# Three score sets of a head pair as two or three stretches of TensorE, and other ranks in the planner

## Chip, cores and metric

One core of one Trainium2 chip runs the whole program in one launch. The metric is the device time of that launch in microseconds (us); below, a lower number is a faster kernel. Engines: PE is TensorE, PEld its weight loads, DVE is VectorE, ACT is ScalarE, POOL is GpSimd, SP is SyncE, which issues the DMAs.

## The reference

Causal attention with a decay, 4 batches x 8 heads, 576 positions, 64 wide, all in float32; then a token mix and a channel mix with residuals; then a gated convolution. Cut to what is computed:

```python
scores = scale * np.matmul(q, k.transpose(0, 1, 3, 2))
cum = np.cumsum(np.log(np.clip(f, 0.0001, 1.0)), axis=-1)
scores = np.where(causal, -1e9, scores + cum[..., :, None] - cum[..., None, :])
attn = softmax(scores)                                   # rows of 576
x = matmul(attn, v)                                      # (4, 576, 512) after joining the heads
u = x + (np.maximum(x.T @ w_tok1, 0.0) @ w_tok2).T       # 256 wide
x2 = u + np.maximum(u @ w_ch1, 0.0) @ w_ch2              # 1536 wide
h = np.maximum(x2 @ w_in, 0.0)                           # 1024 wide
out = (h * sigmoid(conv3(h, conv_w))) @ w_out
```

## The kernel before, in words

**An order made by a planner.** Nearly all work is handed to `Order.add` (called `T`) as tasks: engine, an estimated duration, a rank, the function that emits the instructions, what it reads and writes, and the PSUM banks it holds (`ring`). `Order.run` plays the tasks through with these estimates. Each engine takes, of the tasks that are ready first, the one with the lowest rank; a rank decides only between tasks that are ready at the same moment. The order that comes out is the order of instructions in each engine's queue, and on the chip each engine works through its queue strictly in that order. Two kinds of PSUM bank are planned: `z` (two, each of two banks) and `w` (four).

**Heads and pairs.** 32 heads are taken in 16 pairs (`pair`, L1126). The ranks of head n lie at n x PER; PER is a number of ranks, not a time. For a pair, `score` (L964) makes the scores in five blocks of query rows (0 to 4, with 64 to 576 columns of keys), the two heads on the two halves of TensorE's rows. They come in three sets: block 4 alone (two z banks, one for each head), blocks 0 and 3 (one z bank for both heads), blocks 1 and 2 (one). In each, the products (L987) are followed by the decay (L991). `smax` (L1005, VectorE) adds the mask and takes the maximum out of a z bank, `sexp` (L1011, ScalarE) the exponential. The banks of block 4 come free with the two heads' `smax` of block 4. In the kernel before, the set of blocks 0 and 3 takes two z banks at once, its own and that of blocks 1 and 2, and the latter set has rank -1e6, so that it follows directly.

**After the scores.** Heads 0 to 7 are transposed by TensorE in float32 (L1044) and multiplied with v in float32 (L1076). From head 8 on the probabilities are split into two float16 halves (L1020 on GpSimd, L1026 on VectorE), transposed by DMA, and multiplied with v in three float16 products (L1081 to L1083). Head 31 goes by TensorE again. `norm` and `xout` (L1088 to L1099) divide by the sums; `x_hi`, `x_lo` make float16 halves.

**Groups and batches.** Four heads are a group: the token mix (`t1`, `t2`, three products at L280 to L282, with transposes at L1228), then a copy and the largest value (L266). Two groups are a batch: its scale (L237 on) is found, and u is split in halves (L591, L594). Then `channel_mix` of part 0 (5 of 12 blocks of 128 channels) for the batch's two chunks may run: first product `w<-uh,w`, halves `r` (L643, L647; nine buffers), second product `w<-r,w`. Its TensorE tasks have ranks of 1000 and more, so they fill what attention leaves. The other 7 blocks, and the gated convolution, run after attention.

**Weights.** Each weight block is loaded, joined from two words (L317 on ScalarE, L321 and L322 on VectorE), squared (L517), and when its set's scale is known, split into halves (L551 on ScalarE, L555 on VectorE). Two staging buffers, `wraw`, are used in the order in which the program names the blocks: token weights t1 (3) and t2 (4), then `c10` (5 blocks of w_ch1) and `c20` (5 of w_ch2) of part 0, then the later sets. TOKR, TOKP, VRANK, SETR, LATER and AVAIL are ranks of these: SETR those of c10 and c20, relative to AVAIL[0] - 30.

Of the kernel before, what the change touches and what calls it, by code (L numbers as in the profile page):

```python
# [143 lines left out]
def fox_moe_kernel(  # L144
# [16 lines left out]
    B, S, H, _ = v.shape  # L161
# [44 lines left out]
    LAST = 1  # L206
    BY_PE = [n < TURNED or n >= NH - LAST for n in range(NH)]

    TOKR, TOKP = 4.0, 5.0
    VRANK = 10.0  # L210
    SETR = ((-15.0, 20.0),)
    LATER = (-60.0, 0.0, 20.0)
    PER = 7.0

    const = ctx.enter_context(tc.tile_pool(name="const", bufs=1))
    work = ctx.enter_context(tc.tile_pool(name="work", bufs=1))
# [68 lines left out]
    pools = {}  # L285
# [12 lines left out]
    T = todo.add  # L298
    serial = [0]

    def turn(tag):

        serial[0] += 1
        return (tag, serial[0])
# [443 lines left out]
    with tc.manual_schedule():  # L748
# [153 lines left out]
        def v_scales(g, rank, reads, pools_):  # L902
            kw = turn("w")
            T("ACT", 1.27, rank, v_squares, g, reads=reads, writes=[("junk",), ("vacc", g % 2)], pools=pools_)
            T("PE", 0.25, rank, v_span, g, reads=[("vacc", g % 2)], writes=[kw], pools=["a1"], ring=[kw])
            T("DVE", 0.7, rank, v_pow, g, reads=[kw], writes=[("vsc", g % 3)], pools=["a1"], ring=[kw])

        def v_tasks(g, rank):
# [4 lines left out]
            if HG * g < FULL:  # L913
                if g:
                    T("SP", 2.0, rank - 6, load_v32, g, writes=keys, moved=3.0, pools=["a3"])
                v_scales(g, rank + VRANK, keys, ["a3", "a1"])
                return
# [41 lines left out]

        SETS = {(4,): DEC4, (0, 3): 0, (1, 2): DEC12}  # L960

        JOINED = ((0, 3), (1, 2))

        def score(p, blocks):  # L964
            t = qk_t[p % QKB]
            halves = [slice(64 * x, 64 * x + 64) for x in range(2)]
# [153 lines left out]
        def x_scale(n):  # L1120
            nc.gpsimd.tensor_scalar(x_of(n), x_of(n), tac[:, 0:1], 0.0, ALU.mult, ALU.add)

        PE_S = {(4,): 1.65, (0, 3): 1.25, (1, 2): 1.25}
        DVE_S = {4: 0.81, 3: 0.69, 2: 0.56, 1: 0.42, 0: 0.29}
        ACT_E = {4: 0.78, 3: 0.67, 2: 0.56, 1: 0.46, 0: 0.34}
        SEG = ((4, 3), (2, 1, 0))  # L1126
# [1 line left out]
        def pair(p):  # L1128
            t0 = 2 * p * PER
            kq = ("qk", p % QKB)  # L1130
            A2, A3, A1 = ["a2"], ["a2", "a3"], ["a1"]
            if p:
                T("SP", 0.4, t0 - 9, load_qk, p, writes=[kq], moved=2.6, pools=A2)
            for blocks in SETS:
                second = blocks == JOINED[1]
                kz = [turn("z") for _ in range(2 if blocks == (4,) else 1)] if not second else [kj]
                if blocks == JOINED[0]:
                    kj = turn("z")
                T("PE", PE_S[blocks], -1e6 if second else t0 + 1, score, p, blocks, reads=[kq], writes=[*kz, ("scores",)],
                  pools=A2 + A1, ring=kz + [kj] if blocks == JOINED[0] else kz)  # L1140
                for x, i in ((x, i) for x in range(2) for i in blocks[::-1]):
                    n = 2 * p + x
                    kt = ("t", n % TB)
                    rank = t0 + x * PER
                    T("DVE", DVE_S[i], rank + 2, smax, n, i, reads=[kz[x % len(kz)]], writes=[(*kt, i), ("m", n % 3, i)],
                      pools=A2 + A1, ring=[kz[x % len(kz)]])
                    T("ACT", ACT_E[i], rank + 3, sexp, n, i, reads=[("m", n % 3, i)], writes=[(*kt, i)], pools=A2)
            for n in (2 * p, 2 * p + 1):
                rank = n * PER
                kt = ("t", n % TB)  # L1150
                g = n // HG
                if BY_PE[n]:
                    for a, blks in enumerate(QUADS):
# [3 lines left out]
                          writes=[kw, ("pth", n % 2, a), ("ptl", n % 2, a)], pools=A2 + A1, ring=[kw])  # L1157
                        if n < FULL:
                            T("DVE" if a == 2 else "ACT", 0.14 + 0.115 * len(blks), rank + 4, ptr_copy, n, a, reads=[kw],
                              writes=[("pth", n % 2, a), ("ptl", n % 2, a)], pools=A2 + ["a3"], ring=[kw])  # L1160
                            continue
                        T("ACT", 0.15 + 0.12 * len(blks), rank + 4, ptr_hi, n, a, reads=[kw], writes=[("pth", n % 2, a)],
                          pools=A2 + ["a3"], ring=[kw])
                        T("DVE", 0.12 + 0.17 * len(blks), rank + 4, ptr_lo, n, a, reads=[kw, ("pth", n % 2, a)],
                          writes=[("ptl", n % 2, a)], pools=A2 + ["a3"], ring=[kw])
                else:
                    for q in range(2):
                        T("POOL", (1.22, 1.05)[q], rank + 4, hi_part, n, q, reads=[(*kt, i) for i in SEG[q]],
                          writes=[("ph", n % 2, q)], pools=A2)
                    T("SP", 1.5, rank + 5, transp, n, 0, reads=[("ph", n % 2, 0), ("ph", n % 2, 1)],  # L1170
                      writes=[("pth", n % 2, a) for a in range(len(QUADS))], moved=2.5, pools=A3)
                    for q in range(2):
                        T("DVE", (1.35, 0.9)[q], rank + 4, lo_part, n, q,
                          reads=[(*kt, i) for i in SEG[q]] + [("ph", n % 2, q)], writes=[("pl", n % 2, q)], pools=A2)
                    T("SP", 1.5, rank + 5, transp, n, 1, reads=[("pl", n % 2, 0), ("pl", n % 2, 1)],
                      writes=[("ptl", n % 2, a) for a in range(len(QUADS))], moved=2.5, pools=A3)
# [3 lines left out]
                for i in ORDER:  # L1180
                    T("PE", (0.22 if n < FULL else 0.1) * len(PVB[i]), rank + 6, pv, n, i, reads=[*kp, *vk], writes=[kw, ("xf", g % 2, n % HG)],
                      pools=["a3"], ring=[kw])
# [4 lines left out]
                  writes=[("xl", n % HG)], pools=A1)  # L1187
# [25 lines left out]
        for j in range(NS):  # L1213
            s0, n = (0, 64) if j == 0 else (64 + 128 * (j - 1), 128)
# [60 lines left out]
        def group(g):  # L1275
            t0 = (HG * g + HG - 1) * PER + 6
            A1 = ["a1"]
# [55 lines left out]
        W1K = [("tokw", "t1", k) for k in range(3)]  # L1333
        W2K = [("tokw", "t2", k) for k in range(2 * KT)]
        v_tasks(0, -8)
        AVAIL = [(H * (b + 1) - 1) * PER + 40 for b in range(B)]
        LATE = 1000.0
        tpw = []
        for name, ws, slots, q, factor in (("t1", tok_w[:3], (9, 10, 11), TOKR, 4.0),
                                           ("t2", tok_w[3:], (9, 10, 11, 12), TOKR + 15.0, 2.0 ** 13)):  # L1340
            n = len(ws)
# [8 lines left out]
        T("DVE", 0.2, TOKR + 15.0 + TOKP * 4, tok_scales, reads=[("pw", "t1"), ("pw", "t2")], writes=[("tac",)], pools=["a1"])  # L1350
        t0 = AVAIL[0] - 30
        at = 0
        for x in range(EARLY):
            n = PARTS_M[x]
            for y, (name, w, factor) in enumerate((("ch1", w_ch1, 4.0), ("ch2", w_ch2, 2.0 ** 13))):
                ms = range(M_AT[x], M_AT[x + 1])
                q = t0 + SETR[x][y]
                pw = weight_set(f"c{y + 1}{x}", [(name, m, (col_block if y == 0 else row_block)(w, m)) for m in ms],
                                list(range(at, at + n)), at - 1 if at else 2 * M1,
                                [q + 2.0 * k for k in range(n)], [q + 2.0 * n + 2.0 * k for k in range(n)], factor)  # L1360
                if y == 0:
                    pws.append([pw])
                else:
                    pws[-1].append(pw)
                at += n
        rts1 = ("r1", 9, [0])

        for g in range(NG):
            for p in range(HG * g // 2, HG * (g + 1) // 2):
                pair(p)  # L1370
            if g + 1 < NG:
                v_tasks(g + 1, (HG * g + 2) * PER)
            group(g)
            if g % GB == GB - 1:
                b = g // GB
                for e in range(2):
                    channel_mix(2 * b + e, 0, AVAIL[b] + e * 14, early_u[2 * b + e], None, rts1, "w", "w", LATE, -20.0)

# [36 lines left out]
        for x in range(EARLY, len(PARTS_M)):  # L1415
            n = PARTS_M[x]
            ms = range(M_AT[x], M_AT[x + 1])
            q = T_END + LATER[x - EARLY]
            pws.append([])
# [7 lines left out]
        for b in range(B):  # L1427
            q = T_2 + 2 * P2 * b
# [182 lines left out]
```

## Time and profile before

| | us |
|---|---|
| median of 3 runs | 718.52 (717.6 to 718.86) |
| the profiled execution, device time | 717.27 |
| its span, first to last instruction | 715.5 |
| TensorE busy in the span | 695.6 (97%) |
| VectorE busy | 506.0 (71%) |
| ScalarE busy | 427.8 (60%) |
| GpSimd busy | 242.3 (34%) |

The busy time of an engine is the time in which at least one of its instructions runs. A timeline row gives the start, the duration, the engine, the line and the operation, what it writes and reads, and in square brackets the idle time ahead of it with what ended it. Matmuls overlap in their records, so what one costs is read from start to start. Shares over the whole span mix stages with different limits; the rows below are by stage.

### The profile page before, as it was taken

To read this page: it belongs to the slowest core of one execution; us is meant where nothing else is said; L and a number is where in the kernel's file an instruction comes from. 1 tells how busy PE (TensorE), PEld (TensorE's weight loads), DVE (VectorE), ACT (ScalarE), POOL (GpSimd) and SP (SyncE) were. 2 spreads that over 40 slices of the span, in tenths; PEclk is the share of its full clock that TensorE was granted. 3 is DMA by queue.
4 is the path that set the end of the run, shared out by engine and by line. 5 is a ranking of instruction groups with operands and counts; after the bars stand their busy time and mean duration, and the time that the engine had idled before them with its cause. 6 is when DMAs were issued, how large, how long until landed. Compare 5 with 4: busy or idle time off the path is not lost.

```text
span 715.5 us, 16392 instructions
## 1 busy us (share of the span) xinstructions
PE 695.6 (97%) x6417; PEld 560.0 (78%) x6417; DVE 506.0 (71%) x1264; ACT 427.8 (60%) x939; POOL 242.3 (34%) x321
## 2 busy tenths in 40 slices
PE   6999888999999999999999999999999999999998
PEld 5889665778877787888888778778878778778786
DVE  5787889989987688446566857435778866875570
ACT  5988776685766545545574544112177766676671
POOL 2247563749363657230000212103023222323240
PEclk9999999999999999999999999999999999999999
DMA  8445869799995969784465864345211111100101
GB/s 209 158 128 166 205 196 258 112 256 242 229 233 149 188 137 214 211 267 134 145 197 130 267 217 146 97 134 160 65 42 59 51 59 35 60 18 26 35 17 51
DMA packets 152973, 101.98 MB, mean 143 GB/s; under 512 B 89984, under 2 KB 145024, under 8 KB 152896
## 3 DMA queue, kind: packets, MB, share of 16 engines
q1 hardware_dynamic: 152896, 100.94, 54.0%
q8 instruction: 50, 0.82, 0.5%
q14 instruction: 27, 0.22, 0.1%
HBM read 57.73 MB, written 23.59 MB: 114 GB/s over the span
## 4 chain that ended last, share of the span: by engine, by line
PE 88%; DVE 7%; ACT 2%; issue 1%; SPq 1%; POOL 1%; DMA 0%; ACTq 0%; POOLq 0%; DVEq 0%
PE w L280 15%; PE w L281 15%; PE w L282 15%; PE z L281 8%; PE z L280 8%; PE z L282 8%; PE z L987 6%; PE w L1076 3%; PE w L1228 2%; PE w L1044 2%; DVE pl L1026 2%; PE z L991 1%; PE w L260 1%; DVE ul L594 1%; PE w L1082 1%; PE w L1081 1%
## 5 line engine op out<-in xcount | busy, mean ns | idle before, releaser
L280 PEld LDWEIGHTS <-w 128*128 128x128 f16 x1280 | 125.2, 98 | 34.6 <-issue 2.4
L282 PEld LDWEIGHTS <-w 128*128 128x128 f16 x1280 | 125.5, 98 | 33.8 <-issue 1.9
L281 PEld LDWEIGHTS <-w 128*128 128x128 f16 x1280 | 125.2, 98 | 32.8 <-issue 1.7
L280 PE MATMUL w<-uh,w 128*128 128x288 f16 x416 | 119.6, 288 | 2.0 <-ACT uh L591 1.1
L281 PE MATMUL w<-ul,w 128*128 128x288 f16 x416 | 119.7, 288 | 1.7 <-DVE ul L594 1.7
L282 PE MATMUL w<-uh,w 128*128 128x288 f16 x416 | 119.6, 288 | 0.0
L275 POOL TENSOR_TENSOR g<-sg,g 128x286 f16<-128x286 f32 (+1 forms) x64 | 55.0, 866 | 150.6 <-ACT g L269 149.7
L1511 DVE SCALAR_TENSOR_TENSOR cv<-hp,cw,cv 128x286 f32<-128x286 f32 (+1 forms) x128 | 75.6, 598 | 38.4 <-ACT cv L1505 36.2
L1011 ACT ACTIVATE t<-t,m 128x192 f32<-128x192 f32 (+4 forms) x160 | 82.2, 553 | 15.7 <-DVE m L1005 14.3
L643 ACT ACTIVATE r<-w 128x288 f16<-128x288 f32 x96 | 39.1, 407 | 86.7 <-PE w L282 86.0
L1005 DVE CUSTOM_DVE_ANT_0 t<-z,mask 128x192 f32<-128x192 f32 (+4 forms) x160 | 70.3, 479 | 13.7 <-PE z L991 13.3
L720 POOL TENSOR_TENSOR p<-p,u 128x288 f32<-128x288 f32 x32 | 26.7, 864 | 149.1 <-DMA p<-p_d 89.7
L647 DVE SCALAR_TENSOR_TENSOR r<-w,r 128x288 f16<-128x288 f32 x96 | 43.4, 453 | 45.3 <-ACT r L643 45.0
L281 PE MATMUL z<-g,w 128*128 128x286 f16 (+1 forms) x256 | 73.3, 286 | 0.0
L280 PE MATMUL z<-g,w 128*128 128x286 f16 (+1 forms) x256 | 73.0, 285 | 0.0
L282 PE MATMUL z<-g,w 128*128 128x286 f16 (+1 forms) x256 | 72.9, 285 | 0.0
L280 PE MATMUL w<-vh,w 128*128 128x288 f16 x224 | 64.1, 286 | 0.0
L281 PE MATMUL w<-vl,w 128*128 128x288 f16 x224 | 64.1, 286 | 0.0
L282 PE MATMUL w<-vh,w 128*128 128x288 f16 x224 | 64.1, 286 | 0.0
L280 PE MATMUL z<-r,w 128*128 128x288 f16 x224 | 64.1, 286 | 0.0
L281 PE MATMUL z<-r,w 128*128 128x288 f16 x224 | 64.1, 286 | 0.0
L282 PE MATMUL z<-r,w 128*128 128x288 f16 x224 | 64.1, 286 | 0.0
(200 smaller groups left out, 1678.2 us busy)
## 6 DMA issues: line engine op xcount, KB each, us to landing
wraw<-in_moe_w_ch_dram SPq DMA_DIRECT2D x24, 512.0 KB, 4.5
qk<-in_qk_dram SPq DMA_DIRECT2D x16, 608.0 KB, 5.1
u_d<-us SPq DMA_DIRECT2D x8, 576.0 KB, 3.3
p_d<-res SPq DMA_DIRECT2D x32, 144.0 KB, 3.0
p<-p_d SPq DMA_DIRECT2D x8, 576.0 KB, 5.1
u<-u_d SPq DMA_DIRECT2D x8, 576.0 KB, 4.9
x_d<-p SPq DMA_DIRECT2D x8, 576.0 KB, 3.1
u<-x_d SPq DMA_DIRECT2D x8, 576.0 KB, 3.9
```

The lines of the kernel that those rows point to most:

```text
L275: nc.gpsimd.tensor_tensor(o, a, b, ALU.subtract)
L280: nc.tensor.matmul(ps, wh, xh, start=(first and i == 0), stop=False)
L281: nc.tensor.matmul(ps, wh, xl, start=False, stop=False)
L282: nc.tensor.matmul(ps, wl, xh, start=False, stop=(last and i == n - 1))
L643: nc.scalar.activation(out=t[:, 0, :], in_=box["z", m], func=AF.Relu)
L647: nc.vector.scalar_tensor_tensor(t[:, 1, :], box["z", m], 0.0, f32(t[:, 0, :]), ALU.max, ALU.subtract)
L720: nc.gpsimd.tensor_tensor(box["p"][:, d], box["p"][:, d], box["u"][:, d], ALU.add)
L987: nc.tensor.matmul(out_[x], t[r, Q0[i]:Q0[i] + 128], t[r, k0:k0 + n], start=first, stop=False)
L1005: nc.vector.tensor_tensor_reduce(to, z_t.pop((n, i)), mk, -0.125, 3e38, ALU.add, ALU.min, m_t[n][0:rows, i:i + 1])
L1011: nc.scalar.activation(out=tt[0:rows, o:o + w], in_=tt[0:rows, o:o + w], func=AF.Exp, bias=m_t[n][0:rows, i:i + 1], scale=-1.0)
L1076: nc.tensor.matmul(o[:, 0:65], p32(n)[:, 128 * blk:128 * blk + 128], vp32_t[g % 2][:, slot, hh, :], start=(j == 0), stop=(j == nb - 1))
L1511: nc.vector.scalar_tensor_tensor(cv, hp_t[m][:, s0 + t:s1 + t], cw[:, t, m:m + 1], cv, ALU.mult, ALU.add)
```

## The change

The set of blocks 1 and 2 loses its rank of -1e6 and the set of blocks 0 and 3 its claim on a second bank: each set is a task of the same rank with its own bank or banks. The planner's estimates for the two sets become 1.5 and 1.4 instead of 1.25 and 1.25. The ranks of token weights, v, weight sets, late sets and heads become other numbers. No instruction is added or taken away.

```diff
-    TOKR, TOKP = 4.0, 5.0
-    VRANK = 10.0
-    SETR = ((-15.0, 20.0),)
-    LATER = (-60.0, 0.0, 20.0)
-    PER = 7.0
+    TOKR, TOKP = 10.0, 4.0
+    VRANK = 14.0
+    SETR = ((-25.0, 20.0),)
+    LATER = (-20.0, 0.0, 20.0)
+    PER = 6.0
...
-        JOINED = ((0, 3), (1, 2))
...
-        PE_S = {(4,): 1.65, (0, 3): 1.25, (1, 2): 1.25}
+        PE_S = {(4,): 1.65, (0, 3): 1.5, (1, 2): 1.4}
...
             for blocks in SETS:
-                second = blocks == JOINED[1]
-                kz = [turn("z") for _ in range(2 if blocks == (4,) else 1)] if not second else [kj]
-                if blocks == JOINED[0]:
-                    kj = turn("z")
-                T("PE", PE_S[blocks], -1e6 if second else t0 + 1, score, p, blocks, reads=[kq], writes=[*kz, ("scores",)],
-                  pools=A2 + A1, ring=kz + [kj] if blocks == JOINED[0] else kz)
+                kz = [turn("z") for _ in range(2 if blocks == (4,) else 1)]
+                T("PE", PE_S[blocks], t0 + 1, score, p, blocks, reads=[kq], writes=[*kz, ("scores",)], pools=A2 + A1,
+                  ring=kz)
...
-        AVAIL = [(H * (b + 1) - 1) * PER + 40 for b in range(B)]
+        AVAIL = [(H * (b + 1) - 1) * PER + 35 for b in range(B)]
...
-                                [q + 2.0 * k for k in range(n)], [q + 2.0 * n + 2.0 * k for k in range(n)], factor)
+                                [q + 2.5 * k for k in range(n)], [q + 2.5 * n + 2.5 * k for k in range(n)], factor)
```

## Rows read from the trace of the kernel before

**Rows 1.** The page: its head, and engines' shares of the chain that ended last.

```profile
span 715.5 us, 16392 instructions
...
PE 88%; DVE 7%; ACT 2%; issue 1%; SPq 1%; POOL 1%; DMA 0%; ACTq 0%; POOLq 0%; DVEq 0%
```

**Rows 2.** By stretch: its length, busy us of PE, PEld, DVE, ACT, POOL; clock, DMA.

```profile
16.00:84.00 68.00, 67.22 (x576) 59.02 (x572) 52.32 (x186) 58.67 (x135) 33.22 (x48) 1.00 0.52 160
84.00:120.00 36.00, 27.55 (x256) 19.76 (x252) 32.72 (x81) 24.56 (x49) 17.18 (x21) 0.91 0.88 209
120.00:300.00 180.00, 178.26 (x2180) 143.27 (x2177) 150.71 (x414) 112.53 (x235) 102.09 (x107) 1.00 0.92 197
300.00:712.00 412.00, 412.00 (x3365) 329.25 (x3363) 261.48 (x560) 222.97 (x505) 84.74 (x116) 1.00 0.35 108
```

**Rows 3.** Timeline of TensorE, 84 to 120 us: starts after idle time; last, pair 6.

```profile
87.76 0.37 PE L281 MATMUL w<-xl,w1h 128*128 128x256 f16 x1 [1.27 <-POOL xl L275]
...
106.49 0.28 PE L280 MATMUL w<-uh,w 128*128 128x288 f16 x1 [1.10 <-ACT uh L591]
...
116.88 1.25 PE L987 MATMUL z<-qk 64*128 64x64 f32 x8 [0.93 <-DVE m L1005]
...
118.99 1.13 PE L987 MATMUL z<-qk 64*128 64x192 f32 x8 [0.63 <-DVE m L1005]
```

**Rows 4.** Timeline of TensorE around the joined stretch of pair 9.

```profile
169.00 0.29 PE L281 MATMUL w<-r,w 128*128 128x288 f16 x1
169.13 0.29 PE L282 MATMUL w<-r,w 128*128 128x288 f16 x1
169.34 1.25 PE L987 MATMUL z<-qk 64*128 64x64 f32 x8
...
170.66 1.03 PE L987 MATMUL z<-qk 64*128 64x192 f32 x8
...
171.84 0.28 PE L280 MATMUL w<-xh,w1h 128*128 128x256 f16 x1
```

**Rows 5.** Timeline of TensorE around the stretch of block 4 of pair 9.

```profile
161.86 0.20 PE L1082 MATMUL w<-vp,pt 128*128 128x64 f16 x1
161.89 0.19 PE L1083 MATMUL w<-vp,pt 128*128 128x65 f16 x1
162.02 1.24 PE L987 MATMUL z<-qk 64*128 64x288 f32 x8
...
163.45 0.30 PE L280 MATMUL w<-uh,w 128*128 128x288 f16 x1
```

**Rows 6.** Timeline of VectorE: the two maxima of block 4, pairs 8 and 9.

```profile
154.29 0.75 DVE L1005 CUSTOM_DVE_ANT_0 t<-z,mask 128x576 f32<-128x576 f32 x1
...
154.96 0.75 DVE L1005 CUSTOM_DVE_ANT_0 t<-z,mask 128x576 f32<-128x576 f32 x1
...
164.38 0.74 DVE L1005 CUSTOM_DVE_ANT_0 t<-z,mask 128x576 f32<-128x576 f32 x1
...
168.52 0.74 DVE L1005 CUSTOM_DVE_ANT_0 t<-z,mask 128x576 f32<-128x576 f32 x1
```

**Rows 7.** Timeline of the weight loads around the joined stretch of pair 9.

```profile
169.01 0.10 PEld L282 LDWEIGHTS <-w 128*128 128x128 f16 x1
169.34 0.52 PEld L987 LDWEIGHTS z<-qk 64*128 64x128 f32 x8 [0.24 <-issue]
```

**Rows 8.** Timeline of VectorE: first and last of c10's five low halves.

```profile
81.80 0.74 DVE L555 SCALAR_TENSOR_TENSOR w<-w,pw_c,w 128x512 f16<-128x512 f32 x1
...
94.40 2.27 DVE L555 SCALAR_TENSOR_TENSOR w<-w,pw_c,w 128x512 f16<-128x512 f32 x1
```

**Rows 9.** Timeline of VectorE: the last of c20's five low halves.

```profile
137.62 0.74 DVE L555 SCALAR_TENSOR_TENSOR w<-w,pw_c,w 128x512 f16<-128x512 f32 x1
```

**Rows 10.** Timeline of TensorE: channel mix before c20 is there, and behind it.

```profile
132.85 0.29 PE L282 MATMUL w<-uh,w 128*128 128x288 f16 x1
...
139.17 0.28 PE L280 MATMUL w<-r,w 128*128 128x288 f16 x1
```

## Prediction

> **What bounds the kernel now.** I read four views, in this order. First the page's head and its chain of work that ended last: the span is 715.5 us and 88% of the chain is TensorE [rows 1]. Then the busy time by stretch [rows 2], where the reader is to see three different kernels in one. From 16 to 84 us (heads 0 to 7, scores, transposes and products in float32) TensorE is busy 67.22 of 68.00 us. From 84 to 120 us it is busy only 27.55 of 36.00 us, its granted clock falls to a mean of 0.91, and VectorE is busy 32.72 us: this is the one stretch behind the start in which VectorE sets the pace. From 120 to 300 us TensorE is back at 178.26 of 180.00 us, because the channel mix of the finished batches (rank 1000 and up, so taken only when nothing else is ready) fills every hole that attention leaves. From 300 to 712 us it is busy without a break. Third, the idle times of TensorE inside 84 to 120 us and what ended them [rows 3]: the token mix of group 1 waits for the low half of its last head, and the first channel mix for the split of batch 0, both of which come through VectorE. Fourth, the score stretches one by one, with the VectorE work that frees their banks.
>
> From this follows how the end moves. Behind 120 us TensorE has a fixed amount of work and almost no idle time, so the end moves by (a) what the change adds to the time TensorE needs for its work, and (b) what it changes in the 8.45 us (36.00 - 27.55) of idle time from 84 to 120 us [rows 2]. A faster VectorE chain behind 120 us is worth nothing by itself: it would only swap filler now for filler later.
>
> **The change part by part.** *The split.* Nothing is added or removed in instructions: the same matmuls, the same maxima, the same banks. Today the set of blocks 0 and 3 takes two z banks at once, and the set of blocks 1 and 2 follows it with rank -1e6, so no other work gets between. In the trace the pair of sets runs from 169.34 to 171.84, 2.50 us, the second starting at 170.66 [rows 4]; the set of block 4 runs from 162.02 to 163.45, 1.43 us [rows 5]. After the change the set of blocks 0 and 3 can start when one bank is free, that is after the first maximum of block 4, and the set of blocks 1 and 2 when the second is free.
>
> What one more stretch costs. Ahead of a stretch the filler's pitch of 0.13 us (169.00 to 169.13) becomes 0.21 us (169.13 to 169.34) [rows 4], and the pitch of 0.03 us of the products becomes 0.13 us (161.89 to 162.02) [rows 5]: an entry of 0.08 to 0.10 us. Entry included, the joined stretch takes 2.50 + 0.09 = 2.59 us and the stretch of block 4 takes 1.43 + 0.09 = 1.52 us. By columns (two passes of products and one of decay), the joined stretch streams 2 x 3 x 512 = 3072 and the other 2 x 3 x 288 = 1728. With a fixed part a for each stretch and c for each column, a + 3072c = 2.59 and a + 1728c = 1.52 give c = 0.000796 and a = 0.14. But the products of block 0 are only 64 columns wide and fill their slots badly; the first set takes 1.32 us and the second, of the same columns, 1.18 us [rows 4], and 0.14 us of that is this width or the entry. Taking it off the joined stretch gives c = 0.00069 and a = 0.32. So a further stretch costs 0.14 to 0.32 us; I take 0.25, nearer to the upper value, since 0.08 to 0.10 us of it is seen at the entry alone and the end of the stretch, where the last columns run out before the filler starts, comes on top. The planner's own prices in the diff go from 2.50 us for both sets to 1.5 + 1.4 = 2.9 us; these are the program's numbers and not measurements, and 0.40 is the upper bound that I keep.
>
> How many of the 16 pairs are really split. That hangs on how far apart the two maxima of block 4 (head 2p, head 2p+1) stand on VectorE. In 8 of the 16 pairs they follow each other by 0.68 to 0.97 us, as at 154.29 and 154.96; in the other 8 they are 1.92 to 7.90 us apart, as at 164.38 and 168.52, with splits of other heads and of the channel mix between [rows 6]. A set takes 1.18 to 1.32 us [rows 4], so in the first 8 the second bank is free before the set of blocks 0 and 3 is through, and the next set mostly follows at once, except where products of an earlier head, which have a lower rank, became ready meanwhile. In the other 8 TensorE goes back to filler. I take 10 splits, bounds 8 and 16: 10 x 0.25 = +2.5 us, from 8 x 0.14 = 1.1 to 16 x 0.40 = 6.4 us. What lies beside it: nothing, where TensorE has no idle time; in 84 to 120 us (pairs 5 and 6), where there is some, it can be hidden.
>
> On these weight loads the trace shows two habits. In the filler the load begins 0.12 us ahead of its matmul (load at 169.01, matmul at 169.13); at the stretch's head the load begins at 169.34, with its matmul [rows 4, 7]. The Trainium skill ("TensorE: Matmul & The Clock Gate", Part 3, The mechanism) says that TensorE pulls a weight load ahead of running matmuls where it goes to another row group or to the background buffer. The trace agrees for the filler and not for the head of a stretch; by the rule the entry would be hidden, and the +2.5 us would shrink towards nothing.
>
> *The split in the stretch where VectorE sets the pace.* In pair 6 TensorE enters the joined stretch at 116.88 after 0.93 us of waiting for the first maximum, and its second set starts at 118.99 after 0.63 us of waiting for the second [rows 3]. Channel mix is ready behind it, but TensorE works in the order of its queue. Split, filler can stand in both holes: at most -1.56 us, at least 0 (if the order puts nothing there); I take -0.5, since only the second hole lies between the two sets.
>
> *The ranks.* A rank decides only between tasks that are ready at the same time, and only relative to the heads, which now lie 6 and not 7 apart. Divided by that, the first weight set of the channel mix starts at head 3.7 (rank 22) instead of 6.3 (rank 44), and the token weights 1.1 to 1.5 heads later. Both share two staging buffers in the order of the program, token weights first, so the first set can't be staged before them and keeps about its place; its conversion, ranked at head 5.8 instead of 7.7, gets ahead of attention work sooner. Today its five low halves stand on VectorE from 81.80 to 96.67 us and take 5.39 us there [rows 8], just ahead of the stretch that lacks TensorE work. If all were moved ahead of 84 us, TensorE's idle time could fall by up to these 5.39 us; if the token weights delay them, nothing is gained or 2 us are lost. I take -0.5. The second set's ranks at its conversion go from heads 12.7 to 13.9 to heads 13.3 to 14.9, so up to one head later. Today its last low half starts at 137.62 [rows 9], the second half of the channel mix starts behind it at 139.17, and the last ready matmul of the first half starts at 132.85 [rows 10] (its output has nine buffers). Behind that wait stand all products of the channel mix, so what is late here is filler: each us of delay costs TensorE what attention alone can't fill. I take +1.0, bounds 0 and +3.
>
> The remaining ranks (the squares of v, the late weight sets, the spacing of batches) move tasks on ScalarE, VectorE and the DMA queue of SyncE, past weight loads and head loads there. They are covered by TensorE's unbroken work from 120 to 712 us [rows 2], and if the cover were gone (filler used up before the next batch is ready) the cost would show as idle time of TensorE there, today 1.74 us in 180. I put them at 0, bounds -1 and +1.5. The start up to 16 us waits for the first loads and stays.
>
> **The sum.** +2.5 - 0.5 - 0.5 + 1.0 = +2.5 us. The profiled execution took 717.27 us, 1.77 us around its span of 715.5; with +2.5 it is 719.8. The three runs have their median at 718.52, 1.25 us above that execution, so the forecast for a median is 718.5 + 2.5 = 721.0 us.
>
> **The rivals.** *Faster:* VectorE's load from 84 to 120 us is the mechanism. If the first weight set's low halves leave it (5.39 us of VectorE work [rows 8]) and filler stands in the holes of pair 6, the idle time of 8.45 us falls by 5 us, and with it about 1.5 us of the half-rate time that a granted clock of 0.91 over 36 us means (0.09 x 36 = 3.2 us of work lost) [rows 2]. With the split's +2.5 that is -4 us: 714.5 us. It decides the sign once more than 2.5 us of idle time goes. For it: the ranks say earlier. Against: the shared staging buffers, and the token weights that are now later.
>
> *No difference:* the change doesn't do what it says. Where both banks are free before TensorE turns to the pair, both sets go one after the other as today; if that holds for all but three pairs, the split costs 3 x 0.25 = 0.75 us and the ranks take it back: 718.5 us. For it: TensorE is often late anyway (in 8 pairs the maxima follow each other at once [rows 6]). Against: the other 8. The same time results if a second entry is free (the Trainium skill's rule above); the entry of 0.08 to 0.10 us in [rows 4, 5] speaks against it.
>
> *Much slower:* the second weight set's conversion a head later leaves TensorE without filler from about 133 us on [rows 9, 10]; 4 us of idle time more on top of the split's +2.5 give 725 us. It decides from the point where the set's last low half comes later than TensorE can be fed by attention.
>
> **How the numbers follow.** Forecast 721.0 us, 718.8 to 723.5, chance 0.50. Faster rival 0.22, no difference 0.17, much slower 0.11. About 0.2% (1.4 us) is what a measurement of this kernel can tell from no change, so under 717.1 is faster and over 719.9 slower. Slower: 0.45 of the forecast's 0.50, all of the 0.11 and 0.02 of the no-difference case, 0.58. Faster: 0.22 and 0.01, 0.23. Same: the rest, 0.19. The range is 714.5 to 725.5: its ends are the faster and the slowest case, and what is left out on either side is about a tenth.
>
> **What would show it.** A step is right if, in the changed kernel, about ten of the sixteen pairs show other TensorE work between the set of blocks 0 and 3 and that of blocks 1 and 2, if each such set alone has a pitch of 0.2 us ahead of it and none of its columns run faster, and if TensorE's busy time up to 300 us grows by 2 to 3 us at the same granted clock. The idle time from 84 to 120 us should stay within 2 us of 8.45; the faster rival shows there, as more busy time and a clock near 1.00, with the first weight set's low halves ahead of 84 us. The slower rival shows as idle time of TensorE between 133 and 150 us, ended by the second weight set. The prediction is wrong if the split pairs number under five, or if the idle time changes by more than the split costs.

## The result and the profile after

The changed kernel takes 724.18 us (723.3 to 726.53) against 718.36 us (717.6 to 718.86) before: 1.0087 times as long, interval 1.006 to 1.0114, so +5.8 us (4.3 to 8.2). The forecast was 721.0 us, slower, with a range to 725.5. The sign and the range hold. The time lies above the 718.8 to 723.5 us that the prediction gave its own case, and the size is more than twice the +2.5 us of the sum.

First the page after: its head, the engines' busy times, and the engines' shares of the chain that ended last [rows 1].

```profile
span 721.5 us, 16388 instructions
...
PE 701.4 (97%) x6417; PEld 561.6 (78%) x6417; DVE 514.5 (71%) x1264; ACT 428.5 (59%) x939; POOL 243.6 (34%) x321
...
PE 85%; DVE 7%; POOL 3%; issue 2%; ACT 1%; SPq 1%; DMA 0%; ACTq 0%; POOLq 0%; DVEq 0%
```

The span grew by 6.0 us and TensorE's busy time by 5.8 (695.6 to 701.4). Nearly all of the loss is thus time in which TensorE has an instruction running, and the number of its instructions is the same.

The windows after, with the columns of [rows 2]:

```profile
16.00:84.00 68.00, 65.15 (x542) 55.66 (x538) 54.51 (x186) 57.48 (x131) 31.42 (x43) 1.00 0.49 151
84.00:120.00 36.00, 31.69 (x295) 23.78 (x296) 33.18 (x80) 27.22 (x54) 22.52 (x27) 0.91 0.88 203
120.00:300.00 180.00, 175.18 (x2067) 138.89 (x2064) 151.19 (x403) 109.39 (x230) 99.28 (x105) 1.00 0.89 195
300.00:712.00 412.00, 411.76 (x3427) 329.70 (x3424) 266.55 (x569) 224.23 (x508) 85.30 (x116) 1.00 0.35 110
```

TensorE's idle time (stretch less its busy column) goes from 0.78 to 2.85 us in 16 to 84, from 8.45 down to 4.31 in 84 to 120, and from 1.74 up to 4.82 in 120 to 300. Summed from the first matmul to the last it is 15.46 us before and 15.78 after. It has moved, and not grown. What is late shows at 300 us: 3475 matmuls are still to do up to the end (3427 of them in the window up to 712), before it was 3365 [rows 2].

Now one split pair, pair 9, on TensorE, to be held against [rows 4]; the brackets give idle time and what ended it.

```profile
167.62 1.21 PE L985 MATMUL z<-qk 64*128 64x64 f32 x7 [2.28 <-DVE m L1003]
...
169.03 0.20 PE L1079 MATMUL w<-vp,pt 128*128 128x65 f16 x1
...
170.40 0.19 PE L1081 MATMUL w<-vp,pt 128*128 128x65 f16 x1
170.52 1.13 PE L985 MATMUL z<-qk 64*128 64x192 f32 x8
171.24 0.64 PE L989 MATMUL z<-dec,sel 64*128 64x512 f32 x2
171.82 0.30 PE L280 MATMUL w<-r,w 128*128 128x288 f16 x1
```

The set of blocks 0 and 3 takes 1.41 us (167.62 to 169.03), then 45 products of an earlier head follow, and the set of blocks 1 and 2 takes 1.30 us (170.52 to 171.82). Together 2.71, where the joined stretch took 2.50 [rows 4]. The second set also has an entry of its own: 0.12 us from the last product (170.40) to the set, where products follow each other at 0.03, so 0.09. A split costs 0.21 + 0.09 = 0.30 us. In the trace 12 of the 16 pairs are split this way and four are still joined (those at 12.23, 154.44, 185.81 and 217.99 us): 12 x 0.30 = 3.6 us.

What TensorE waited for from 16 to 400 us (engine, tile and line that waits, what it waits for; us in all, times, longest), first before, then after. These lists name the visible idle time only.

```profile
PE w L281 <- DVE ul L594: 1.7, 1, 1.7
PE w L281 <- POOL xl L275: 1.7, 2, 1.3
PE w L280 <- ACT xh L269: 1.6, 1, 1.6
PE z L987 <- DVE m L1005: 1.6, 2, 0.9
```

```profile
PE z L985 <- DVE m L1003: 8.4, 6, 2.8
PE w L260 <- ACT junk L872: 2.4, 1, 2.4
...
PE w L281 <- POOL xl L275: 0.4, 2, 0.2
```

Before, TensorE waited mostly for the halves that feed the token mix and the channel mix. After, it waits for VectorE's maxima ahead of score sets: 1.6 us became 8.4, in six places. The wait at 167.62 above is one. VectorE's timeline ahead of it:

```profile
162.81 1.33 DVE L322 SCALAR_TENSOR_TENSOR w<-w,wraw 128x512 int32<-128x512 int32 x1
164.06 2.47 DVE L1024 SCALAR_TENSOR_TENSOR pl<-t,ph 128x1024 f16<-128x1024 f32 x2
...
166.75 0.72 DVE L1003 CUSTOM_DVE_ANT_0 t<-z,mask 128x576 f32<-128x576 f32 x1
```

The maximum that frees the bank stands behind the join of a weight block and two splits of probabilities. TensorE's queue has the score set in front, and the 45 products stand behind it; whether they could have run in these 2.28 us is not shown.

The largest wait of the list, on TensorE's timeline, then the VectorE row that makes the low halves of u (`ul`):

```profile
111.43 1.76 PE L985 MATMUL z<-qk 64*128 64x64 f32 x7 [2.83 <-DVE m L1003]
...
113.62 0.42 PE L280 MATMUL w<-uh,w 128*128 128x288 f16 x1
```

```profile
111.20 2.27 DVE L594 SCALAR_TENSOR_TENSOR ul<-us,su,uh 128x576 f16<-128x576 f32 x3
```

The work next in the queue, the channel mix at 113.62, reads `ul` from its second matmul (L281) on, and VectorE makes `ul` only from 111.20 on. So at most one matmul behind the set could have run in the 2.83 us: the set didn't hold up filler here, the filler wasn't ready.

And the window behind the wait, with the columns of [rows 2]:

```profile
112.00:115.40 3.40, 3.40 (x14) 1.57 (x11) 3.15 (x9) 1.64 (x3) 0.20 (x1) 0.50 1.12 275
```

After 2.83 us of idle time the granted clock is 0.50, 1.2 of 2.4 GHz, for 3.4 us, and the set takes 2.19 us (111.43 to 113.62) instead of 1.41. Not every such wait is followed by it: behind 2.28 us at 167.62 the mean clock stays 1.00 (the window from 120 to 300). Before, 10.2 us of the span lie at half clock, after 13.7. Counting half of TensorE's busy time there as lost, that is 4.94 and 5.83 us: +0.9. This holds for the two profiled executions; two others of the changed kernel, of 724.9 and 726.53 us, had a mean granted clock of 0.986 instead of 0.991, so this share differs from execution to execution.

One more part is hidden in the busy time, a wait inside a score set. The set of block 4 at 104.69:

```profile
104.69 0.75 PE L985 MATMUL z<-qk 64*128 64x288 f32 x2
105.93 0.76 PE L985 MATMUL z<-qk 64*128 64x288 f32 x4 [0.49 <-DVE m L1003]
...
107.33 0.49 PE L260 MATMUL w<-ident,um 128*128 128x128 f32 x2
```

It takes 2.64 us (to 107.33) where such a set took 1.43 [rows 5], at a granted clock of 1.00. It begins with one bank and waits for the second; of the 1.2 us more only 0.49 show as idle, since the matmul records ahead of the wait run on. So 0.7 us of waiting count as busy. Four smaller ones (65.65, 151.20, 160.37 and 224.93 us) add about 0.8, and before had 0.3 to 0.4 of the kind (149.56, 116.88): about +1.1 net.

Together 3.6 (12 splits) + 0.9 (half clock) + 1.1 (waits inside score sets) + 0.3 (idle) = 5.9 of the span's 6.0 us. The 1.1 is read set by set and good to some tenths.

### The profile page after: what moved, and what is told of

Its sections match the earlier page's. It is cut to its first block, busy times and chain, and to the rows that moved or that the text cites. A ratio compares the mean times of both kernels' runs of the same rounds, so it can differ in the third digit from the quotient of the medians.

```text
span 721.5 us, 16388 instructions
## 1 busy us (share of the span) xinstructions
PE 701.4 (97%) x6417; PEld 561.6 (78%) x6417; DVE 514.5 (71%) x1264; ACT 428.5 (59%) x939; POOL 243.6 (34%) x321
## 4 chain that ended last, share of the span: by engine, by line
PE 85%; DVE 7%; POOL 3%; issue 2%; ACT 1%; SPq 1%; DMA 0%; ACTq 0%; POOLq 0%; DVEq 0%
PE w L280 14%; PE w L281 14%; PE w L282 14%; PE z L281 8%; PE z L280 8%; PE z L282 8%; PE z L985 6%; PE w L1074 3%; DVE pl L1024 2%; PE w L1042 2%; DVE t L1003 2%; PE w L1223 2%; PE z L989 1%; PE w L260 1%; PE w L1080 1%
## 5 line engine op out<-in xcount | busy, mean ns | idle before, releaser
L281 PEld LDWEIGHTS <-w 128*128 128x128 f16 x1280 | 125.2, 98 | 31.6 <-issue 0.6
L281 PE MATMUL w<-ul,w 128*128 128x288 f16 x416 | 119.3, 287 | 0.1
L275 POOL TENSOR_TENSOR g<-sg,g 128x286 f16<-128x286 f32 (+1 forms) x64 | 55.1, 867 | 150.4 <-ACT g L269 148.6
L1009 ACT ACTIVATE t<-t,m 128x448 f32<-128x448 f32 (+4 forms) x160 | 82.6, 552 | 21.3 <-DVE m L1003 21.2
L1003 DVE CUSTOM_DVE_ANT_0 t<-z,mask 128x448 f32<-128x448 f32 (+4 forms) x160 | 71.1, 478 | 10.5 <-PE z L989 10.5
L281 PE MATMUL z<-g,w 128*128 128x286 f16 (+1 forms) x256 | 73.3, 286 | 0.0
L985 PE MATMUL z<-qk 64*128 64x288 f32 (+4 forms) x384 | 63.0, 438 | 9.6 <-DVE m L1003 8.4
L281 PE MATMUL w<-vl,w 128*128 128x288 f16 x224 | 64.1, 286 | 0.0
L280 PE MATMUL z<-r,w 128*128 128x288 f16 x224 | 64.1, 286 | 0.0
L281 PE MATMUL z<-r,w 128*128 128x288 f16 x224 | 64.1, 286 | 0.0
```

What stands on the lines that cost most here:

```text
L275: nc.gpsimd.tensor_tensor(o, a, b, ALU.subtract)
L280: nc.tensor.matmul(ps, wh, xh, start=(first and i == 0), stop=False)
L281: nc.tensor.matmul(ps, wh, xl, start=False, stop=False)
L985: nc.tensor.matmul(out_[x], t[r, Q0[i]:Q0[i] + 128], t[r, k0:k0 + n], start=first, stop=False)
L1003: nc.vector.tensor_tensor_reduce(to, z_t.pop((n, i)), mk, -0.125, 3e38, ALU.add, ALU.min, m_t[n][0:rows, i:i + 1])
L1009: nc.scalar.activation(out=tt[0:rows, o:o + w], in_=tt[0:rows, o:o + w], func=AF.Exp, bias=m_t[n][0:rows, i:i + 1], scale=-1.0)
```

## The experiments

The question: which part of the +5.8 us is the price of a split, which the ranks, and are these two separable at all? "Before" is the kernel before, timed beside each on the same chip.

| kernel | median us | before, us | ratio (interval) | pairs split |
|---|---|---|---|---|
| e1_broken | 722.86 | 718.10 | 1.0071 (1.0059 to 1.0083) | 16, by one matmul |
| e2_ahead | 718.11 | 718.10 | 1.0002 (0.9994 to 1.0011) | 0 |
| e3_split_old_ranks | 740.58 | 718.10 | 1.0317 (1.0292 to 1.0342) | 9 |
| e4_joined_new_ranks | 733.25 | 718.10 | 1.0212 (1.0199 to 1.0225) | 0 |
| e5_split_old_per | 733.65 | 717.16 | 1.0219 (1.0155 to 1.0283) | 10 |
| e6_split_old_tok | 738.43 | 717.16 | 1.029 (1.0267 to 1.0312) | 9 |
| e7_split_old_set | 729.13 | 717.16 | 1.0152 (1.0121 to 1.0183) | 12 |
| e8_joined_estimates | 730.43 | 717.16 | 1.0176 (1.0155 to 1.0197) | 0 |
| e9_joined_tokr | 741.33 | 718.33 | 1.032 (1.0294 to 1.0346) | 0 |
| e10_no_claim | 727.39 | 718.33 | 1.012 (1.0093 to 1.0147) | 3 |
| e11_split_late_banks | 727.26 | 718.33 | 1.0135 (1.0102 to 1.0167) | 8 |
| e12_split_old_later | 726.2 | 718.33 | 1.0109 (1.0084 to 1.0134) | 12 |

**The price of a break by itself.** e1_broken leaves before's order as it is and puts one small float16 matmul on zeros between the two joined sets of every pair. e2_ahead, its control, has the same matmul ahead of the joined sets.

```diff
+        gap = const.tile([128, 128], F16, name="gap")
+        nc.gpsimd.memset(gap, 0.0)
...
+            if blocks == JOINED[1]:      # e2_ahead: JOINED[0]
+                nc.tensor.matmul(z[:, 0, 0:64], gap, gap[:, 0:64], start=True, stop=True)
```

> The kernel before with one float16 matmul of 64 columns, on zeros, put between the set of blocks 0 and 3 and that of blocks 1 and 2 of each of the 16 pairs; it writes into the bank ahead of the products, which start it anew, so nothing computed changes, and the planner's order is that of before. Theory (a further stretch costs about 0.30 us, as the changed kernel's rows give: first set 1.41 instead of 1.32, second 1.30 instead of 1.18, entry 0.09): 16 x 0.30 and 16 matmuls of 0.03 us, about +5.3 us, 723.6 us. Rival (the weight loads of the second stretch are hidden, the changed kernel lost its time through its order): +0.5 us for the matmuls alone, 718.9 us.

> The control for the broken stretch: the same 16 float16 matmuls, one ahead of the set of blocks 0 and 3, where other work stands anyway, so that no stretch is broken. Both theories: 16 x 0.03 = +0.5 us, 718.9 us; clearly more would mean that the extra matmul itself, or its wait for the bank, costs.

Measured: e1_broken +4.8 us, the control 0.0. TensorE in e1_broken, a joined pair now broken (its scores are at L991 and L995), then the weight load of its second set:

```profile
160.53 1.25 PE L991 MATMUL z<-qk 64*128 64x64 f32 x8
161.26 0.75 PE L995 MATMUL z<-dec,sel 64*128 64x512 f32 x2
161.94 0.20 PE L988 MATMUL z<-gap 128*128 128x64 f16 x1
162.07 1.13 PE L991 MATMUL z<-qk 64*128 64x192 f32 x8
162.80 0.64 PE L995 MATMUL z<-dec,sel 64*128 64x512 f32 x2
163.37 0.30 PE L280 MATMUL w<-r,w 128*128 128x288 f16 x1
```

```profile
162.07 0.63 PEld L991 LDWEIGHTS z<-qk 64*128 64x128 f32 x8
```

1.41, then 0.13 for the small matmul and the entry, then 1.30: the 1.41 and 1.30 of the split pair above. The matmul itself is free in the control, so the whole difference is the break: (722.86 - 718.11) / 16 = 0.30 us each (0.26 to 0.37 by the interval of the ratio). The span of this execution also holds 20.5 us at half clock instead of 10.2 and 1.6 us less idle time, so the quotient alone isn't clean; that it agrees with the rows is what settles the price. The Trainium skill ("TensorE: Matmul & The Clock Gate", Part 3, The mechanism) has a weight load pulled ahead of running matmuls where it goes to another row group that doesn't conflict, or to the background buffer. Here the load of the second set starts at 162.07, with its matmul, and the entry is paid. This need not go against the rule: the 64 rows of a score load lie among the 128 of the matmul ahead, so it may be neither case, and no run here settles that.

**Structure and ranks, two by two.** e3_split_old_ranks is the changed kernel with all of before's ranks. e4_joined_new_ranks is the kernel before, joined and with its own estimates, with all ranks of the changed one.

```diff
# e3_split_old_ranks, against the changed kernel (e4_joined_new_ranks: the reverse, against the kernel before)
-    TOKR, TOKP = 10.0, 4.0
-    VRANK = 14.0
-    SETR = ((-25.0, 20.0),)
-    LATER = (-20.0, 0.0, 20.0)
-    PER = 6.0
+    TOKR, TOKP = 4.0, 5.0
+    VRANK = 10.0
+    SETR = ((-15.0, 20.0),)
+    LATER = (-60.0, 0.0, 20.0)
+    PER = 7.0
...
-        AVAIL = [(H * (b + 1) - 1) * PER + 35 for b in range(B)]
+        AVAIL = [(H * (b + 1) - 1) * PER + 40 for b in range(B)]
...
-                                [q + 2.5 * k for k in range(n)], [q + 2.5 * n + 2.5 * k for k in range(n)], factor)
+                                [q + 2.0 * k for k in range(n)], [q + 2.0 * n + 2.0 * k for k in range(n)], factor)
```

> The three sets as three tasks, with the planner's estimates of the change, but all ranks of the kernel before. Its order has 9 of 16 pairs with other work between the two sets (the changed kernel 12). Theory (price of the stretches): 9 x 0.30 = +2.7 us, 721.1 us, with the idle time of TensorE as before. Rival (the ranks alone did it): 718.4 us. Second rival (the order that the split makes costs by itself): 723 us or more, as idle time.

> The joined stretch of the kernel before with all ranks of the change; no pair has other work between the two sets. Theory (price of the stretches, 3.6 of the 5.8 us): the other 2.2 us stay, 720.6 us. Rival (the ranks alone did it): 724 us. If the split is all of it: 718.4 us.

Measured: +22.5 and +15.2 us. The split alone costs 22.5, the ranks alone 15.2, both together 5.8. So they don't add, and the ranks, which the prediction put at nothing or a little, are worth -16.4 us once the sets are split (740.6 to 724.2). Where the time goes: the window from 84 to 220 us, before, after, e3_split_old_ranks, e4_joined_new_ranks in this order.

```profile
84.00:220.00 136.00, 126.38 (x1388) 97.93 (x1385) 123.94 (x331) 92.03 (x189) 78.68 (x85) 0.97 0.94 215
```

```profile
84.00:220.00 136.00, 127.47 (x1384) 98.67 (x1384) 123.05 (x319) 91.73 (x187) 81.37 (x88) 0.97 0.92 213
```

```profile
84.00:220.00 136.00, 118.31 (x1251) 91.70 (x1250) 121.25 (x315) 86.05 (x176) 77.88 (x85) 0.91 0.94 212
```

```profile
84.00:220.00 136.00, 121.40 (x1306) 94.22 (x1305) 123.96 (x326) 90.89 (x187) 74.99 (x81) 0.94 0.97 219
```

Both odd kernels lose 5 to 8 us of TensorE's busy time there and have a lower mean clock; VectorE's busy time is within 3 us of before's. In the lists of waits the maxima lead, in e3_split_old_ranks and then in e4_joined_new_ranks:

```profile
PE z L985 <- DVE m L1003: 9.9, 4, 4.1
```

```profile
PE z L987 <- DVE m L1005: 11.4, 5, 4.0
```

**Is it one group of ranks?** Four kernels put one group back in the changed kernel: e5_split_old_per PER and AVAIL, e6_split_old_tok the token weights and v, e7_split_old_set the first weight sets and their spacing, e12_split_old_later the late sets.

```diff
# e5_split_old_per
-    PER = 6.0
+    PER = 7.0
-        AVAIL = [(H * (b + 1) - 1) * PER + 35 for b in range(B)]
+        AVAIL = [(H * (b + 1) - 1) * PER + 40 for b in range(B)]
# e6_split_old_tok
-    TOKR, TOKP = 10.0, 4.0
-    VRANK = 14.0
+    TOKR, TOKP = 4.0, 5.0
+    VRANK = 10.0
# e7_split_old_set, and a spacing of 2.0 instead of 2.5
-    SETR = ((-25.0, 20.0),)
+    SETR = ((-15.0, 20.0),)
# e12_split_old_later
-    LATER = (-20.0, 0.0, 20.0)
+    LATER = (-60.0, 0.0, 20.0)
```

> The changed kernel with the spacing of heads (PER 7 and the +40 of AVAIL) of before; all else as changed. The split with all ranks of before took 740.6 us, with all ranks of the change 724.2, so the ranks are worth 16 us to the split, and this run asks which. Theory (the spacing of heads sets which work of the next pair goes ahead of this pair's, so it carries most of it): 735 us or more, with TensorE stalled ahead of score sets. Rival (the token weights carry it): about 724 us.

> The changed kernel with the ranks of the token weights and of v (TOKR, TOKP, VRANK) of before. Theory (the spacing of heads carries the 16 us): about 724 to 727 us. Rival (the token weights, which come ahead of all other weight sets in the two staging buffers, carry it): 735 us or more.

> The changed kernel with the ranks of the first two weight sets of the channel mix (SETR -15 and the spacing of 2.0) of before. Theory of the prediction (these ranks are worth 0.5 us here): 724 us. Rival (no one group of ranks carries the 16 us; each departure from a set of ranks that was fitted together costs some us): 728 us or more, as idle time and half clock of TensorE between 84 and 220 us.

> The changed kernel with the rank of the late weight sets (LATER -60) of before; all else as changed. The prediction put this rank at 0. Theory of the fitted order: some us slower than the changed kernel, 726 us or more. Theory of the prediction: 724 us.

Measured against before: +16.5, +21.3, +12.0 and +7.9 us, all above the +5.8 with all the new ranks. Each group put back gives a longer median, though e12_split_old_later isn't clear of the changed kernel (+6.0 to +9.6 us by its interval against +4.3 to +8.2). The excess over the changed kernel (10.7, 15.5, 6.2 and 2.1) adds up to 34 us where all of them together are worth 16.4. No single group carries it, and they don't add among themselves either. The times of e5_split_old_per spread from 728.9 to 738.2 us; its size is the least certain.

**A control for the ranks.** If the new ranks mattered by their sense, a change without sense should do nothing. e8_joined_estimates changes only the planner's two estimates in the kernel before, no rank and no instruction. e9_joined_tokr moves one rank by 0.2, which breaks a tie. e10_no_claim drops only the claim on the second bank and leaves the rank of -1e6.

```diff
# e8_joined_estimates, against the kernel before
-        PE_S = {(4,): 1.65, (0, 3): 1.25, (1, 2): 1.25}
+        PE_S = {(4,): 1.65, (0, 3): 1.5, (1, 2): 1.4}
# e9_joined_tokr, against the kernel before
-    TOKR, TOKP = 4.0, 5.0
+    TOKR, TOKP = 4.2, 5.0
# e10_no_claim, against the kernel before
-                kz = [turn("z") for _ in range(2 if blocks == (4,) else 1)] if not second else [kj]
-                if blocks == JOINED[0]:
-                    kj = turn("z")
+                kz = [turn("z") for _ in range(2 if blocks == (4,) else 1)]
...
-                  pools=A2 + A1, ring=kz + [kj] if blocks == JOINED[0] else kz)
+                  pools=A2 + A1, ring=kz)
```

> The kernel before, joined, with its own ranks; only the planner's estimates of the two sets are those of the change (1.5 and 1.4 instead of 1.25 and 1.25). No instruction and no rank differs, only what the planner believes. Theory (the order is fitted; any change of what goes into the plan moves it away from an order that the chip follows without stalls): 721 us or more, with stalls of TensorE that the kernel before doesn't have. Rival (what counts is the ranks' sense, and a small change of an estimate is worth nothing): 718 us.

> The kernel before with TOKR 4.2 instead of 4.0, nothing else: a rank too small a step to have a meaning (heads lie 7 apart), but it breaks a tie between the first token weight and the transposes of head 0, and the orders of all engines differ from there on. Theory (the orders are fitted; where a change of the plan leads can't be told from its sense): 722 us or more, as idle time and half clock between 84 and 220 us. Rival (only ranks moved far, as by the change, cost): 717 to 719 us.

> One part of the change alone: the set of blocks 0 and 3 claims only its own bank, but the set of blocks 1 and 2 keeps its rank of -1e6 and all ranks and estimates are those of before. 3 of the 16 pairs are then split. By the price of a stretch alone: 3 x 0.30 = +0.9 us, 718 to 719 us. By the theory of the fitted order: 722 us or more, most of it idle time and half clock, not stretches.

Measured: +13.3, +23.0 and +9.1 us. A tie broken the other way costs as much as the split under the old ranks. The orders of all three differ from before's through the attention. e10_no_claim really splits three pairs, 0.9 us by the price above; the rest is its order. One wait of e9_joined_tokr on TensorE's timeline:

```profile
132.76 1.33 PE L987 MATMUL z<-qk 64*128 64x288 f32 x4 [4.86 <-DVE m L1005]
```

And VectorE's timeline ahead of its end:

```profile
129.25 0.81 DVE L1026 SCALAR_TENSOR_TENSOR pl<-t,ph 128x640 f16<-128x640 f32 x1
129.98 1.01 DVE L321 TENSOR_SCALAR wraw<-wraw 128x512 int32<-128x512 int32 x1
131.10 0.83 DVE L322 SCALAR_TENSOR_TENSOR w<-w,wraw 128x512 int32<-128x512 int32 x1
131.85 0.48 DVE L1005 CUSTOM_DVE_ANT_0 t<-z,mask 128x320 f32<-128x320 f32 x1
```

As at 167.62 in the changed kernel, and at twice the size, the maximum stands behind splits and joins on VectorE. Not every order stalls there. In e8_joined_estimates the first waits are for the token mix (4.0 us on L275, 3.3 on L269).

**Is the planner too early with the banks?** It takes a z bank as free 0.1 us after the end that it planned for the last maximum. e11_split_late_banks, the changed kernel with 1.5 us instead, should then put other work ahead of the score sets.

```diff
-                    at = max(at, until[held[place]] + 0.1)
+                    at = max(at, until[held[place]] + (1.5 if x[0] == "z" else 0.1))
```

> The changed kernel with one thing different in the planner: it takes a z bank for free 1.5 us after its last maximum instead of 0.1 us, so it puts filler ahead of a score set whose bank comes late on the chip. 8 pairs are split instead of 12. Theory (the changed kernel's new idle time is TensorE standing at the head of its queue ahead of a score set that the plan put there too early): TensorE's waits for maxima fall from 8.4 us to under 4 us; the time depends on where the rest of the order falls, 720 to 730 us. Rival (the waits come from VectorE's pace, whatever the order): 8 us of such waits or more stay.

Measured: 727.26 us, +8.9 on before. Its list of waits:

```profile
PE w L281 <- POOL xl L275: 6.7, 5, 2.1
PE w L281 <- DVE ul L594: 2.8, 2, 2.6
PE w L280 <- ACT xh L269: 1.8, 2, 1.0
PE w L280 <- ACT uh L591: 1.7, 1, 1.7
```

The waits on maxima, 8.4 us in the changed kernel, are gone from this list (part is hidden: the set of block 4 at 166.34 takes 2.00 us instead of 1.43), and 13 us of waits for the halves of the two mixes stand in their place. The expectation came true, but its theory doesn't follow from that, since other orders move these waits too: with the 0.1 us kept they are 1.6 us in the kernel before and 11.4 in e4_joined_new_ranks. And it gained nothing.

The plan itself speaks against the theory. `Order.run` of the changed kernel, played through with its estimates (the program's numbers, not measurements), already has TensorE idle ahead of the same sets: 2.84 us ahead of the set at 111.43, 1.43 at 138.49, 0.71 at 167.62, and 0.54 each at 84.69 and 104.69, together 6.1 of the 8.4 us. A planned idle time means that by the estimates no other task was ready. Only some 2 us, most of it at 167.62, are left for banks that the chip frees later than planned.

The planner's own end of the whole order is a test of the same kind. It is 718.4 us for the kernel before and 718.9 for the changed one; 737.6 (e3), 733.3 (e4), 732.5 (e5), 735.5 (e6), 733.8 (e7), 740.4 (e8), 738.4 (e9), 727.2 (e10), 734.9 (e11) and 724.7 (e12). All but e8 and e11, which it puts 10.0 and 7.6 us too high, lie within 5.3 us of the measured median; 6.4 us of e8's 10.0 are its raised estimates (16 x 0.4) for stretches that are still joined. So what other ranks cost stands for the most part in the plan already, as work that isn't ready in time, before the chip adds anything of its own.

No version is faster than the kernel before.

## Why the prediction was right, and where it was not

**The bound.** Right: what ends the program is TensorE's need of time plus its idle time, and VectorE's chain by itself counts for nothing. TensorE's busy time explains 5.8 of the 6.0 us.

**The split: mechanism right, size too small.** Forecast 10 x 0.25 = 2.5, measured 12 x 0.30 = 3.6 us. The price lies near the upper of the two fits (0.32), the one that takes the narrow products of block 0 out of the price of a column; 0.25 went too far down towards the other. The count went by the distances of the maxima in the old order. That a hidden entry would let the +2.5 us "shrink towards nothing" was too wide: the entry is 0.09 of the 0.30 us.

**The stretch where VectorE sets the pace: wrong sign.** The -0.5 us stood on filler in the second of pair 6's two holes. That hole did go (its set, now at 125.35, doesn't wait), but the first, for which the prediction allowed nothing worse than no gain, grew from 0.93 us [rows 3] to 2.83 and was followed by half clock. The step took it that filler is ready behind a hole. At 111.43 it wasn't: the channel mix was waiting for `ul`, and the plan has 2.84 us of idle time in the same place.

**The first weight set: moved as said, and given back.** Its low halves now start at 78.03 instead of 81.80 [rows 8]. The idle time from 84 to 120 us fell by 4.1 us, where the prediction said it would stay within 2 us; that part of the faster rival came true. But 2.1 us more idle time stand from 16 to 84 (one wait at 83.15, for ScalarE's L872) and 3.1 more from 120 to 300. The rival had counted the gain in one stretch and taken the others as fixed.

**The second weight set: late as said, but no wait on it.** Its last low half went from 137.62 [rows 9] to 142.24, the second half of the channel mix from 139.17 [rows 10] to 148.54. The forecast was +1.0 us. TensorE's idle time in between is 1.43 us, and a maximum ends it, not the weight set, so as a wait the term measured nothing:

```profile
138.49 1.25 PE L985 MATMUL z<-qk 64*128 64x64 f32 x8 [1.43 <-DVE m L1003]
...
148.48 0.20 PE L1080 MATMUL w<-vp,pt 128*128 128x64 f16 x1
148.51 0.19 PE L1081 MATMUL w<-vp,pt 128*128 128x65 f16 x1
148.54 0.28 PE L280 MATMUL w<-r,w 128*128 128x288 f16 x1
```

Scores, token mix and products filled the rest. So the much slower rival, whose 725 us is the nearest number, is not what happened: its 4 us of idle time up to 150 us aren't there.

**The remaining ranks: the step that failed.** They stood at 0, bounds -1 and +1.5, "covered by TensorE's unbroken work". Idle time from 120 to 300 us is the sign that the prediction named for a lost cover, and it rose by 3.1 us. By the runs the ranks can't be priced by their sense at all: +15.2 us with the joined sets, -16.4 with the split ones, and 23.0 for a tie. The planner's own end tells most of it: +19.2 us for the split alone, +14.9 for the ranks alone and +0.5 for both, measured 22.5, 15.2 and 5.8. The sum came out near because the new ranks suit the new structure: of two terms of about 20 us with opposite signs, neither of which stood in the sum, about 2 us were left over, as half clock and as waits inside score sets. That is luck in the sum, though not in its first term.

**A test that couldn't work.** The prediction wanted TensorE's busy time up to 300 us to grow by 2 to 3 us. Up to a fixed time busy and idle make one sum, so with the same idle time it can't grow. What grows is the work left at that time, the 3475 matmuls against 3365.

**Open.** Why just this order stalls where it does was not followed back to single estimates; only the bank's 0.1 us was tried. For the change the plan has 6.4 us more work and 5.9 us less idle time of TensorE, where the chip shows 3.6 us for the splits and 0.3 us more idle time; why the planned gain is missing isn't known. That before's and the changed kernel's ranks are each fitted to their structure is inferred from the neighbours, which are slower in time and in the planner's own end. Whether other ranks would bring the split below 718 us wasn't tried.

## What to carry to other kernels

Price a broken stretch by breaking it in place, with the same instruction beside it as a control, before reasoning about queues. Where a planner makes the order, its ranks and estimates form one set with the structure: read the planner's own end and its planned idle time first, then run structure and ranks two by two, and with them a change that means nothing, since here that alone moved the time by 23 us. Follow idle time over the whole span, as it can leave one stretch and stand in another at the same total.

## What the runs showed of the hardware

Leaving a stretch of 64-row float32 matmuls and coming back costs 0.30 us, 0.09 of it at the entry, even for one float16 matmul of 64 columns that is free elsewhere.

Half clock adds to what a stall costs. The orders of e3, e4, e6, e8 and e9 have 27.3 us (e3_split_old_ranks) to 34.1 us (e9_joined_tokr) of the span at 1.2 GHz where before has 10.2; in e9_joined_tokr that is 8.9 us of lost work on top of 13.4 us more idle time, of +24.4 in the span. It isn't part of every longer order: e11_split_late_banks, 8.9 us above before, has 10.2 us of it like before. Nor does the order alone decide it: executions of e5_split_old_per took 728.94 and 730.07 us at mean granted clocks of 0.993 and 0.995, and 737.23 and 738.15 us at 0.976 and 0.978.

A matmul's record runs on while the next of its set waits for a bank: of the 1.2 us that the set at 104.69 in the changed kernel lost, 0.49 show as idle time. Idle time alone undercounts such waits; what a set takes from start to start shows them.
